# The last head of a cached-attention decode step in single-column products, with the output as four rows

## The chip, the cores and the metric

The kernel runs on one core of a Trainium2 chip. The metric is the device time of one execution in microseconds; each kernel was run several times, and medians are quoted. The profile's span is about 1.8 us shorter than the quoted time of the same execution in nearly all runs. All positions ("at 2511.9 us") are microseconds from the start of a span.

## The reference, cut to what matters

One token attends to a cache of 65,536 keys and values in each of 32 heads; a small gated feed-forward block is mixed in.

```python
B, Sq, D = 1, 1, 512
H, Sk, Dh = 32, 65536, 128              # k_cache, v_cache: (1, 32, 65536, 128) bf16, 512 MiB each

q = (x @ wq) in heads
p = softmax(einsum("bhqd,bhkd->bhqk", q, k_cache) * Dh**-0.5)
a = einsum("bhqk,bhkd->bhqd", p, v_cache) -> (1, 1, H*Dh) @ wo
b = (silu(x @ w_gate) * (x @ w_up)) @ w_down
g = sigmoid((x * gate_w).sum(-1))
out = g * a + (1 - g) * b               # (1, 1, 512)
```

## The kernel before

K and V stream through three slots of 8 MB in SBUF. Each head has two chunks (`CH = 2`), so there are 64 chunks, 0 to 63; chunks 62 and 63 are the last head. For a chunk, VectorE multiplies K by the broadcast q, TensorE (PE) sums over the head dimension with an identity as stationary operand ("score sums"), ScalarE takes the exponentials. Then V is weighted in one of two ways.

For all chunks but the very last, the probabilities are stationary, four columns at a time, and V streams through as 512 columns. That gives a 4 x 512 result of which four 1 x 128 pieces are wanted; `diagonal` picks them:

```python
    def pv(n):
        ...
        last = CH - 2 if h == H - 1 else CH - 1
        mms(("pv", s, n % 2, c == 0, c == last), O_ps,
            [(P_sb[n % 2][:, g : g + VB], v[:, g : g + VB, :].rearrange("p a b -> p (a b)"))
             for g in range(0, KPP, VB)], ...)          # 64 products of 512 columns
        if c == last:
            act("O_sb", O_sb, O_ps, ACT.Copy, ["O_ps"], ["O_sb"])
            pending.append(h)
```

For chunk 63 V itself is stationary and one column of probabilities streams through, 256 times; V arrives in five pieces, so the work can follow the loads. Then comes the end of the kernel:

```python
    V_END = [KPP // 2, KPP // 4, KPP // 8, KPP // 16, KPP // 16]    # 128, 64, 32, 16, 16 columns
    ...
    load("k", n, [EK] * (KPP // EK))
    load("v", n, V_END)
    turn_outputs(1)
    rows("b_ps", wd, ..., hT, "hT", range(FT))          # 56 single-column products
    diagonal()
    for i, j in enumerate(range(0, KPP, EK)):           # the last four blocks of scores
        block(n, j, EK)
        if i == 0:
            ...
            rows("a_ps", wo, ..., M, "M", range(H))     # 128 single-column products
        ...
    for m in V_END:
        mms(("c", at), m_c[:, 0:1],
            [(v[:, j, :], P_sb[n % 2][:, j : j + 1]) for j in range(at, at + m)], ...)
        if at == 0:
            norm(h, H)
        at += m
    dve("o_last", lambda: nc.vector.tensor_scalar_mul(o_last, m_c[:, 0:1], tot[:, h:H]), ...)
    rows("l_ps", wo_last, ..., o_last, "o_last", [0])   # 4 single-column products
    dve("out_sb", ...)                                  # [128, 4]
    dma("out", out[0, 0].rearrange("(p b) -> p b", b=OT), out_sb, ["out"], ["out_sb"])
```

The projections read their weights with a stride of four elements, so that the 512 outputs stand as 128 partitions x 4, and the output leaves as 128 pieces of 8 bytes:

```python
    def rows(key, w_v, names, cols, cname, ks):
        ... [(w_v[:, k, bass.ds(b, P, OT)], cols[:, k : k + 1]) for k in ks] ...   # b in 0..3
```

The softmax here doesn't subtract the row's maximum and nothing guards it: scores larger than these inputs give would overflow.

## Time and profile before

| before | value | where |
|---|---|---|
| time, first 3 runs | 2521.22 us median (2519.79 to 2521.41) | runs |
| DMA | 1088 MB at 432 GB/s, 99.7% of 16 engines' span | page, part 3 |
| last score sum starts | 2506.13 us | timeline |
| last piece of V landed | 2511.90 us | semaphore records |
| last single-column product starts | 2514.50 us | timeline |
| output issued, landed | 2515.62, 2518.59 us | timeline, semaphore records |

The kernel is a stream of loads with work behind it. So the reading starts with the DMA queues, from the page of the kernel before (queue and kind: packets, MB, share of the 16 engines' span):

```profile
span 2519.9 us, 15461 instructions
...
DMA packets 20903, 1088.04 MB, mean 432 GB/s; under 512 B 2450, under 2 KB 2580, under 8 KB 2836
## 3 DMA queue, kind: packets, MB, share of 16 engines
q1 hardware_dynamic: 20880, 1087.78, 99.7%
q8 instruction: 13, 0.21, 0.0%
```

The stream fills the engines. What a change at the end can win is the time from the last landing to the end. This is the last stretch of the chain of waits before (start, length, what; times in us):

```profile
2503.27 3.24 PE S_ps_102 L269 x15
2506.51 3.19 PE m_c L251 x128
2509.70 0.23 PE m_x L251 x2
2509.93 1.51 PE m_c L251 x58
2511.44 1.22 issue
2512.66 2.02 PE m_c L251 x70
...
2514.71 0.23 DVE o_last L588
...
2515.07 0.28 PE m_x L279 x4
...
2515.38 0.22 DVE out_sb L593
```

The first three lines say that PE was late: its score sums ended at 2506.5, when the first 128 columns of V had been there since 2502.2, and the 128 products that need them came only then. The line "1.22 issue" is a pause in the middle of a run of equal products; no semaphore ends it. The last V piece landed during that pause (2511.90), and 2.6 us later PE started its last product. The wait of the queue that issued the output, from the waits view (waited for: us in total, times, longest):

```profile
SPq L179 <- DMA out_dram<-out_sb: 2.6, 1, 2.6
```

With the issue itself that is 2.97 us from issue to landing, for 1 KB.

### The profile page before, as it was taken

The numbers are of one execution on the slowest core, as the hardware profiler recorded it, in microseconds if no ns is written. First come the engines' busy times: TensorE is split into PE (matmuls) and PEld (weight loads), VectorE is DVE, ScalarE is ACT, GpSimd is POOL, SyncE is SP. The second block draws the span as 40 slices with busy tenths as digits, with TensorE's granted clock in tenths as the row PEclk, the third lists the DMA queues.
The fourth block names the chain that finished last, engine by engine and source line by source line (L and its number), as shares of the span: only waits on it lengthen the run. The fifth ranks groups of instructions, "written<-read, shape, count | busy, mean of one in ns | idle before, by whom it ended". The sixth has DMA issues, their size and how long they took to land.

```text
span 2519.9 us, 15461 instructions
## 1 busy us (share of the span) xinstructions
PE 1980.9 (79%) x9115; PEld 410.4 (16%) x5153; DVE 1268.7 (50%) x290; ACT 97.9 (4%) x402; POOL 1.9 (0%) x9
## 2 busy tenths in 40 slices
PE   4787877877878778778787787787787877877888
PEld 1111111111111111111111111111111111111113
DVE  3455455464554554644645536446455455464454
ACT  0000000000000000000000000000000000000000
POOL 0000000000000000000000000000000000000000
PEclk8888988989889889899899899898988988989998
DMA  9999999999999999999999999999999999999998
GB/s 423 431 432 433 434 435 435 433 435 437 433 434 433 434 433 435 436 436 433 434 435 435 433 434 433 434 434 437 434 436 433 434 437 433 434 433 433 433 431 361
DMA packets 20903, 1088.04 MB, mean 432 GB/s; under 512 B 2450, under 2 KB 2580, under 8 KB 2836
## 3 DMA queue, kind: packets, MB, share of 16 engines
q1 hardware_dynamic: 20880, 1087.78, 99.7%
q8 instruction: 13, 0.21, 0.0%
q14 instruction: 6, 0.05, 0.0%
q10 hardware_dynamic: 4, 0.00, 0.0%
HBM read 1087.77 MB, written 0.00 MB: 432 GB/s over the span
## 4 chain that ended last, share of the span: by engine, by line
DMA 44%; PE 41%; DVE 13%; ACT 1%; issue 0%; another core or an unknown queue 0%; SPq 0%; DVEq 0%; ACTq 0%
PE O_ps L251 18%; DMA slot_67<-in_A_k_cache_dram 16%; DMA slot_65<-in_A_k_cache_dram 14%; DMA slot_66<-in_A_k_cache_dram 14%; PE S_ps_101 L269 11%; PE S_ps_102 L269 9%; DVE slot_67 L338 4%; DVE slot_66 L338 4%; DVE slot_65 L338 3%; DVE S_sb_82 L363 2%; PE m_c L251 1%; PE S_ps_101 L279 1%; PE m_x L279 1%; ACT P_sb_83 L288 1%; DMA slot_65<-in_A_wq_dram 0%; PE S_ps_102 L279 0%
## 5 line engine op out<-in xcount | busy, mean ns | idle before, releaser
L338 DVE TENSOR_TENSOR slot_67<-slot_67,q_bc_79 128x16384 bf16<-128x16384 bf16 (+1 forms) x28 | 208.2, 7469 | 143.8 <-DMA slot_67<-in_A_k_cache_dram 143.8
L363 DVE TENSOR_REDUCE S_sb_82<-S_ps_102 128x128 f32<-128x1024 f32 (+1 forms) x67 | 78.8, 1177 | 392.8 <-PE S_ps_102 L269 392.8
L338 DVE TENSOR_TENSOR slot_65<-slot_65,q_bc_78 128x16384 bf16<-128x16384 bf16 x22 | 190.2, 8689 | 146.9 <-DMA slot_65<-in_A_k_cache_dram 146.9
L338 DVE TENSOR_TENSOR slot_66<-slot_66,q_bc_78 128x16384 bf16<-128x16384 bf16 (+1 forms) x24 | 190.6, 7978 | 136.7 <-DMA slot_66<-in_A_k_cache_dram 121.2
L338 DVE TENSOR_TENSOR slot_66<-slot_66,q_bc_79 128x16384 bf16<-128x16384 bf16 x20 | 172.9, 8689 | 119.9 <-DMA slot_66<-in_A_k_cache_dram 119.9
L338 DVE TENSOR_TENSOR slot_65<-slot_65,q_bc_79 128x16384 bf16<-128x16384 bf16 x20 | 172.9, 8689 | 119.1 <-DMA slot_65<-in_A_k_cache_dram 119.1
L338 DVE TENSOR_TENSOR slot_67<-slot_67,q_bc_78 128x16384 bf16<-128x16384 bf16 x20 | 172.9, 8689 | 117.3 <-DMA slot_67<-in_A_k_cache_dram 117.3
L269 PE MATMUL S_ps_101<-slot_67,ident 128*128 128x512 bf16 x680 | 191.3, 450 | 0.0
L269 PE MATMUL S_ps_101<-slot_65,ident 128*128 128x512 bf16 x651 | 187.1, 458 | 0.0
L269 PE MATMUL S_ps_101<-slot_66,ident 128*128 128x512 bf16 x650 | 185.3, 455 | 0.0
L251 PE MATMUL O_ps<-slot_67,P_sb_83 128*4 128x512 bf16 x704 | 155.9, 383 | 27.9 <-ACT P_sb_83 L288 18.3
L251 PE MATMUL O_ps<-slot_65,P_sb_83 128*4 128x512 bf16 x704 | 155.2, 381 | 19.6 <-ACT P_sb_83 L288 19.6
L251 PE MATMUL O_ps<-slot_66,P_sb_84 128*4 128x512 bf16 x704 | 153.7, 379 | 19.3 <-ACT P_sb_84 L288 19.3
L251 PE MATMUL O_ps<-slot_65,P_sb_84 128*4 128x512 bf16 x640 | 139.7, 379 | 18.3 <-ACT P_sb_84 L288 18.3
L251 PE MATMUL O_ps<-slot_67,P_sb_84 128*4 128x512 bf16 x640 | 139.7, 379 | 18.3 <-ACT P_sb_84 L288 18.3
L251 PE MATMUL O_ps<-slot_66,P_sb_83 128*4 128x512 bf16 x640 | 139.7, 379 | 17.5 <-ACT P_sb_83 L288 17.5
L269 PE MATMUL S_ps_102<-slot_67,ident 128*128 128x512 bf16 x680 | 152.4, 382 | 0.0
L269 PE MATMUL S_ps_102<-slot_65,ident 128*128 128x512 bf16 x651 | 143.9, 379 | 0.0
L269 PE MATMUL S_ps_102<-slot_66,ident 128*128 128x512 bf16 x650 | 143.9, 379 | 0.0
L279 PE MATMUL S_ps_101<-slot_65,ident 128*128 128x512 bf16 x21 | 12.8, 608 | 134.5 <-DVE slot_65 L338 134.5
L279 PE MATMUL S_ps_101<-slot_66,ident 128*128 128x512 bf16 x22 | 13.1, 597 | 130.5 <-DVE slot_66 L338 130.5
L279 PE MATMUL S_ps_101<-slot_67,ident 128*128 128x512 bf16 x24 | 13.9, 580 | 125.4 <-DVE slot_67 L338 125.4
(89 smaller groups left out, 702.8 us busy)
## 6 DMA issues: line engine op xcount, KB each, us to landing
slot_66<-in_A_k_cache_dram SPq DMA_DIRECT2D x4, 2048.0 KB, 24.5
slot_67<-in_A_k_cache_dram SPq DMA_DIRECT2D x4, 2048.0 KB, 29.0
slot_65<-in_A_wq_dram SPq DMA_DIRECT2D x1, 4096.0 KB, 12.3
slot_66<-in_A_wo_dram SPq DMA_DIRECT2D x1, 4096.0 KB, 32.5
slot_65<-in_A_v_cache_dram SPq DMA_DIRECT2D x1, 4096.0 KB, 20.5
slot_65<-in_A_v_cache_dram SPq DMA_DIRECT2D x1, 2048.0 KB, 24.9
slot_65<-in_B_w_gate_dram SPq DMA_DIRECT2D x1, 1792.0 KB, 34.7
slot_65<-in_B_w_up_dram SPq DMA_DIRECT2D x1, 1792.0 KB, 38.4
```

What stands on the lines that cost most here:

```text
L251: ins = nc.tensor.matmul(out_ap, lhsT=a, rhs=b, start=start and i == 0, stop=stop and i == len(pairs) - 1,)
L269: ins = nc.tensor.add_instruction(mybir.InstMatmult(name=nc.get_next_instruction_name(), engine=mybir.EngineType.PE, ins=[nc.tensor.lower_ ...
L279: ins = nc.tensor.matmul(out_ap, lhsT=a, rhs=b, start=first, stop=last)
L288: "ACT", key, lambda: nc.scalar.activation(out=out_ap, in_=in_ap, func=func, **kw),
L338: "products", lambda: nc.vector.tensor_tensor(out=w, in0=w, in1=q_rep, op=ALU.mult),
L363: lambda: nc.vector.tensor_reduce(out=S_sb[b][:, :m], in_=S_ps[r][:, :m, :], axis=AXIS.X, op=ALU.add),
```

## The change

Intent: let PE finish sooner after the last landing, and let V's slot come free sooner. Four things change. (1) Chunk 62 is done in single-column products too, in three groups, and accumulates with chunk 63, so the last head has no diagonal. (2) Both projections move ahead of the last score sums. (3) The output is four rows of 128 (256 bytes each): the scaled last head is copied into four columns of a 128 x 16 zero matrix `Z` (column q of the q-th block of four), four products of 128 columns give a 4 x 128 result, and the part that was ready earlier is transposed to that shape ahead of time. (4) As a consequence the projections read contiguous weights. The diff also moves the row sums and the normalization of the earlier heads within the programs of PE and VectorE.

```diff
+    rest4 = sb("rest4", [OT, P], f32)
+    ident_f = sb("ident_f", [P, P], f32)
+    Z = sb("Z", [P, OT * OT], bf16)
-    out_sb = sb("out_sb", [P, OT], bf16)
+    out_sb = sb("out_sb", [OT, P], bf16)
...
-                    [(w_v[:, k, bass.ds(b, P, OT)], cols[:, k : k + 1]) for k in ks],
+                    [(w_v[:, k, P * b : P * (b + 1)], cols[:, k : k + 1]) for k in ks],
...
-        pv(n)
+        if n < N - 2:
+            pv(n)
+        else:
+            column(n, [KPP // 2, KPP // 4, KPP // 4])
...
+    turn_outputs(0)
     turn_outputs(1)
-    rows("b_ps", wd, units(ws, 0, WO), hT, "hT", range(FT))
-    diagonal()
+    rows("b_ps", wd, units(ws, 0, WO), hT, "hT", range(FT), m_x, "m_x")
+    rows("a_ps", wo, units(ws, WO, WL), M, "M", range(H), m_sp, "m_sp")
     for i, j in enumerate(range(0, KPP, EK)):
...
+            mms("rest_ps", m_sp[:OT, :P], [(rest, ident_f)], ["rest", "ident_f"], ["m_sp"])
+            act("rest4", rest4, m_sp[:OT, :P], ACT.Copy, ["m_sp"], ["rest4"])
...
-    rows("l_ps", wo_last, units(ws, WL, WL + D), o_last, "o_last", [0])
+    mms(
+        "l_ps", m_x[:OT, :P],
+        [(Z[:, OT * q : OT * (q + 1)], wo_last[:, 0, P * q : P * (q + 1)]) for q in range(OT)],
+        ["Z"] + units(ws, WL, WL + D), ["m_x"],
+    )
...
-    dma("out", out[0, 0].rearrange("(p b) -> p b", b=OT), out_sb, ["out"], ["out_sb"])
+    dma("out", out[0, 0].rearrange("(i p) -> i p", p=P), out_sb, ["out"], ["out_sb"])
```

More of the change, by code (lines that the diff above doesn't have):

```diff
@@ L148 @@
     rest = sb("rest", [P, OT], f32)
+    rest4 = sb("rest4", [OT, P], f32)
+    ident_f = sb("ident_f", [P, P], f32)
+    Z = sb("Z", [P, OT * OT], bf16)
     o_row = sb("o_row", [H, Dh], bf16)
     M = sb("M", [P, H], bf16)
-    o_last = sb("o_last", [P, 1], bf16)
-    out_sb = sb("out_sb", [P, OT], bf16)
+    out_sb = sb("out_sb", [OT, P], bf16)
     S_ps = [psum.tile([P, HK, R], f32, name=f"S_ps{i}") for i in range(2)]
@@ L226 @@
     op("DVE", "oT0", lambda: nc.vector.memset(oT, 0.0), writes=["oT"])
+    op("DVE", "Z0", lambda: nc.vector.memset(Z, 0.0), writes=["Z"])
     op("DVE", "rowsum0", lambda: nc.vector.memset(rowsum, 0.0), writes=["rowsum"])
@@ L239 @@
     select("ident", ident, ones_b, "ones_b", [[-1, P]], 1)
+    select("ident_f", ident_f, ones, "ones", [[-1, P]], 1)
     select("pick", pick, ones[0:VB, 0:VB], "ones", [[-1, VB]], 1)
@@ L381, in pv @@
         s = where["v", n]
-        last = CH - 2 if h == H - 1 else CH - 1
         v = view(s, 0, KPP, Dh)
         mms(
-            ("pv", s, n % 2, c == 0, c == last), O_ps,
+            ("pv", s, n % 2, c == 0, c == CH - 1), O_ps,
             [
@@ L393, in pv @@
             [("P_sb", n % 2, u) for u in range(RS)] + units(s, 0, SLOT), ["O_ps"],
-            start=(c == 0), stop=(c == last),
+            start=(c == 0), stop=(c == CH - 1),
         )
-        if c == last:
+        if c == CH - 1:
             act("O_sb", O_sb, O_ps, ACT.Copy, ["O_ps"], ["O_sb"])
@@ L403, in diagonal, with column @@
         mms(
-            ("diagonal", h == H - 1), m_c[:, 0:1],
+            "diagonal", m_c[:, 0:1],
             [(O_sb[:, j * Dh : (j + 1) * Dh], pick[:, j : j + 1]) for j in range(VB)],
-            ["O_sb", "pick"], ["m_c"], stop=(h < H - 1),
+            ["O_sb", "pick"], ["m_c"],
         )
-        if h < H - 1:
-            act("o_all", o_all[:, h : h + 1], m_c[:, 0:1], ACT.Copy, ["m_c"], [("o_all", h)])
+        act("o_all", o_all[:, h : h + 1], m_c[:, 0:1], ACT.Copy, ["m_c"], [("o_all", h)])
+    def column(n, pieces, at=0):
+        s = where["v", n]
+        v = view(s, 0, KPP, Dh)
+        for m in pieces:
+            mms(
+                ("c", n, at), m_c[:, 0:1],
+                [(v[:, j, :], P_sb[n % 2][:, j : j + 1]) for j in range(at, at + m)],
+                [("P_sb", n % 2, u) for u in range(at // EK, -(-(at + m) // EK))]
+                + units(s, at * Dh, (at + m) * Dh),
+                ["m_c"], start=(n == N - 2 and at == 0), stop=(n == N - 1 and at + m == KPP),
+            )
+            at += m
     def hidden():
@@ L456, in gate, with rows @@
         )
-    def rows(key, w_v, names, cols, cname, ks):
+    def rows(key, w_v, names, cols, cname, ks, bank, bname):
         group(
@@ L463, in rows @@
                 (
-                    m_x[:, b : b + 1],
-                    [(w_v[:, k, bass.ds(b, P, OT)], cols[:, k : k + 1]) for k in ks],
+                    bank[:, b : b + 1],
+                    [(w_v[:, k, P * b : P * (b + 1)], cols[:, k : k + 1]) for k in ks],
                 )
@@ L468, in rows, with sum_ps @@
             ],
-            names + [cname], ["m_x"],
+            names + [cname], [bname],
         )
-    def norm(h0, h1):
+    def sum_ps(h0, h1):
         w = CH * RS
@@ L475, in norm @@
             ["ones", "rowsum"] + [("rowsum", i) for i in range(h0 * w, h1 * w)], ["m_x"])
+    def norm(h0, h1):
+        w = CH * RS
         dve(
@@ L523 @@
         for j in range(0, KPP, m):
+            if n == N - 2 and j == 2 * m:
+                sum_ps(0, H - 1)
             block(n, j, m)
@@ L529 @@
                     diagonal()
-            elif n == N - 2 and j + m == KPP:
-                norm(0, H - 1)
-                outputs()
             while len(todo) > 1:
@@ L539 @@
         if n == N - 2:
-            turn_outputs(0)
-        pv(n)
+            norm(0, H - 1)
+            outputs()
+        if n < N - 2:
+            pv(n)
+        else:
+            column(n, [KPP // 2, KPP // 4, KPP // 4])
     n, h = N - 1, H - 1
@@ L553 @@
     load("v", n, V_END)
+    turn_outputs(0)
     turn_outputs(1)
-    rows("b_ps", wd, units(ws, 0, WO), hT, "hT", range(FT))
-    diagonal()
+    rows("b_ps", wd, units(ws, 0, WO), hT, "hT", range(FT), m_x, "m_x")
+    rows("a_ps", wo, units(ws, WO, WL), M, "M", range(H), m_sp, "m_sp")
     for i, j in enumerate(range(0, KPP, EK)):
-        block(n, j, EK)
-        if i == 0:
+        if i == 1:
             dve("rest", lambda: nc.vector.tensor_scalar_mul(rest, m_x[:, :OT], ngval),
                 ["m_x", "ngval"], ["rest"])
-            rows("a_ps", wo, units(ws, WO, WL), M, "M", range(H))
-        if i == 2:
             dve(
@@ L566 @@
                 lambda: nc.vector.scalar_tensor_tensor(
-                    out=rest, in0=m_x[:, :OT], scalar=gval, in1=rest, op0=ALU.mult, op1=ALU.add
+                    out=rest, in0=m_sp[:, :OT], scalar=gval, in1=rest, op0=ALU.mult, op1=ALU.add
                 ),
-                ["m_x", "gval", "rest"], ["rest"],
+                ["m_sp", "gval", "rest"], ["rest"],
             )
+        if i == 2:
+            mms("rest_ps", m_sp[:OT, :P], [(rest, ident_f)], ["rest", "ident_f"], ["m_sp"])
+            act("rest4", rest4, m_sp[:OT, :P], ACT.Copy, ["m_sp"], ["rest4"])
+        block(n, j, EK)
         while len(todo) > 1:
@@ L573 @@
     gather()
-    s = where["v", n]
-    v = view(s, 0, KPP, Dh)
-    at = 0
-    for m in V_END:
-        mms(
-            ("c", at), m_c[:, 0:1],
-            [(v[:, j, :], P_sb[n % 2][:, j : j + 1]) for j in range(at, at + m)],
-            [("P_sb", n % 2, u) for u in range(at // EK, -(-(at + m) // EK))]
-            + units(s, at * Dh, (at + m) * Dh),
-            ["m_c"], start=False, stop=(at + m == KPP),
-        )
-        if at == 0:
-            norm(h, H)
-        at += m
-    dve("o_last", lambda: nc.vector.tensor_scalar_mul(o_last, m_c[:, 0:1], tot[:, h:H]),
-        ["m_c", ("tot", h)], ["o_last"])
-    rows("l_ps", wo_last, units(ws, WL, WL + D), o_last, "o_last", [0])
+    column(n, V_END[:1])
+    sum_ps(h, H)
+    norm(h, H)
+    column(n, V_END[1:], V_END[0])
+    dve(
+        "Z",
+        lambda: nc.vector.tensor_scalar_mul(
+            Z[:, :: OT + 1], m_c[:, 0:1].to_broadcast([P, OT]), tot[:, h:H]
+        ),
+        ["m_c", ("tot", h)], ["Z"],
+    )
+    mms(
+        "l_ps", m_x[:OT, :P],
+        [(Z[:, OT * q : OT * (q + 1)], wo_last[:, 0, P * q : P * (q + 1)]) for q in range(OT)],
+        ["Z"] + units(ws, WL, WL + D), ["m_x"],
+    )
     dve(
@@ L593 @@
         lambda: nc.vector.scalar_tensor_tensor(
-            out=out_sb, in0=m_x[:, :OT], scalar=gval, in1=rest, op0=ALU.mult, op1=ALU.add
+            out=out_sb, in0=m_x[:OT, :P], scalar=gval[:OT, :], in1=rest4,
+            op0=ALU.mult, op1=ALU.add,
         ),
-        ["m_x", "gval", "rest"], ["out_sb"],
+        ["m_x", "gval", "rest4"], ["out_sb"],
     )
-    dma("out", out[0, 0].rearrange("(p b) -> p b", b=OT), out_sb, ["out"], ["out_sb"])
+    dma("out", out[0, 0].rearrange("(i p) -> i p", p=P), out_sb, ["out"], ["out_sb"])
     op("SP", "end", None, reads=["out"])
```

## The prediction

> **What bounds the kernel.** DMA. The page's DMA-queue part: 1088 MB at a mean 432 GB/s, the queue's packets filling 99.7% of the 16 engines; the slice row shows DMA at 9 in every slice but the last. PE is 79% busy and DVE 50%, but neither sets the pace. The change moves no byte out of this stream, so only what follows the last V landing, or starves the stream, can change the time.
>
> **The end of it, from the timeline, the windows and the semaphore records.** The last five pieces of V land at 2502.20, 2507.04, 2509.47, 2510.69 and 2511.90 us. PE is behind them: its last score sums start at 2502.9 and end at 2506.5, because 128 projection products (4.4 us, from 2488.2) and a half-clock stretch stood in front of the second block. It then does 256 single-column products at about 26 ns each, and pauses inside them: the chain of waits shows 1.22 us of "issue" from 2511.44, a pause that no semaphore ends. The DMA records have a 16,384-byte instruction packet from 2510.31 to 2511.24. The Trainium skill ("Runtime: NRT & Kernel Launch", Instruction fetch mechanics) says an engine's instructions come in 16 KiB blocks of 256 through the sequencer's own DMA queue; so I read the pause as an instruction fetch (inferred, not shown). The last product therefore starts at 2514.50, 2.6 us after the last V landing. Then: scaling (0.22), four products, final sum (0.22), issue at 2515.62, landing at 2518.59 (2.97 us), end at 2519.9.
>
> **What the change does, costed.**
> - Chunk 62: 64 products of 512 columns (15.5 us, 2466.2 to 2481.7) become 256 single-column products, estimated 6.7 us at 26 ns. V's slot comes free about 8 us earlier, so the last V loads are issued earlier. Worth about 0: the queue was already full (DMA share near 1.0 from 2460 to 2508).
> - The projections (1.9 and 4.4 us) move ahead of the last sums, into a hole where PE waits for K. The last sums should end at 2500.5 to 2504.5, and the first columns wait for V rather than V for them.
> - The diagonal (1.0 us) goes; a small transpose comes, off the path.
> - About 370 more PE instructions (384 added for chunk 62, 16 removed): the block boundary moves. An estimate by 256s puts it near the start of the second column group, where PE waits for V anyway, and the next near the last four products. It also means one or two more fetches, each of which delays one DMA engine by about 0.9 us (the spread of a landing grew from 2.0 to 3.1 us after the fetch at 2447); I expect other engines than the latest ones, so no later last landing.
> - End: last product at about 2512.5 (-2.0). Four products of 128 columns at half clock and a final sum over 128 elements instead of 4: +0.4. Output as four rows of 256 B instead of 128 pieces of 8 B: -0.5, a guess; most of the 2.97 us is the write's receipt (the skill's "DMA: Bandwidth & Descriptors", Anatomy of one DMA, says the same).
>
> Sum: about -2.1 us, 2519.1 us. This is 0.1%.
>
> **What would show it.** Chain of waits: no "issue" piece inside the last columns; DMA landing, then 16 columns. Last V landing still at 2511.9 +- 0.3. Last column to output issue 1.5 us (1.12 before). Output landing 2.2 to 2.7 us.
>
> **What would make it wrong.** A fetch pause in the last 32 columns or before the last four products (+1 to +2 us); a fetch hitting the latest DMA engine (+0.9); the scatter of the three runs before (1.6 us) is as large as the gain.
>
> Chances: faster by over 2% 0.005, within 2% 0.99, slower 0.005. 2519.1 us, range 2517.2 to 2521.0.

## More of the kernel before

PE's program is a loop over heads 1 to 30, three heads a round; head 0 and the last head are written out.

## The result, and the profile after

| | before | after |
|---|---|---|
| time, 4 runs each | 2521.18 us median (2519.79 to 2521.41) | 2518.43 us median (2518.11 to 2518.69) |
| span of the profile | 2519.9 us | 2517.0 us |
| last score sum starts | 2506.13 | 2501.54 |
| last piece of V issued, landed | 2483.52, 2511.90 | 2471.53, 2512.55 |
| last single-column product starts | 2514.50 | 2513.02 |
| output issued, landed | 2515.62, 2518.59 | 2514.50, 2515.69 |

The ratio of the fast runs is 0.999 (95% interval 0.9973 to 1.0008): the same at the 2% that counts here. Ratios are the mean time of one kernel's fast runs over the mean of the other's fast runs of the same rounds, so they are not quite the ratio of the medians quoted. The 2.75 us between the medians is small but larger than the scatter of the runs after, and the slowest run after is below the fastest run before. The runs after also scatter less: 0.6 us against 1.6 us.

The page after:

```profile
span 2517.0 us, 15837 instructions
...
DMA packets 20769, 1088.07 MB, mean 432 GB/s; under 512 B 2314, under 2 KB 2444, under 8 KB 2700
## 3 DMA queue, kind: packets, MB, share of 16 engines
q1 hardware_dynamic: 20744, 1087.78, 99.8%
q8 instruction: 15, 0.25, 0.0%
```

The stream is as full as before, and two more blocks of instructions were fetched (15 packets against 13). The end of the chain of waits after:

```profile
2471.53 41.02 DMA slot_65<-in_A_v_cache_dram
2512.55 0.05 issue
2512.60 0.60 PE m_c L255 x16
...
2513.23 0.24 DVE Z L606
...
2513.51 0.60 PE m_x L255 x4
...
2514.14 0.34 DVE out_sb L618
```

The chain now hangs on the load of V: it lands at 2512.55, then come 16 columns (0.60), the scaling (0.24), four products (0.60) and the final sum (0.34). No "issue" piece stands inside the last columns any more. The output's wait in the waits view:

```profile
SPq L181 <- DMA out_dram<-out_sb: 0.8, 1, 0.8
```

That is 1.19 us from issue to landing in place of 2.97. Of the 2.9 us between the two spans, 1.1 us is the earlier issue and 1.8 us the faster landing.

### The profile page after: what moved, and what is told of

It reads as the page before. It is cut to its first block, busy times and chain, and to the rows that moved or that the text cites. A ratio compares the mean times of both kernels' runs of the same rounds, so it can differ in the third digit from the quotient of the medians.

```text
span 2517.0 us, 15837 instructions
## 1 busy us (share of the span) xinstructions
PE 1966.3 (78%) x9301; PEld 409.7 (16%) x5339; DVE 1268.6 (50%) x291; ACT 97.8 (4%) x402; POOL 2.2 (0%) x10
## 3 DMA queue, kind: packets, MB, share of 16 engines
q1 hardware_dynamic: 20744, 1087.78, 99.8%
## 4 chain that ended last, share of the span: by engine, by line
DMA 46%; PE 39%; DVE 13%; ACT 1%; issue 1%; another core or an unknown queue 0%; SPq 0%; DVEq 0%; ACTq 0%
PE O_ps L255 17%; DMA slot_67<-in_A_k_cache_dram 16%; DMA slot_65<-in_A_k_cache_dram 14%; DMA slot_66<-in_A_k_cache_dram 14%; PE S_ps_103 L273 10%; PE S_ps_104 L273 8%; DVE slot_67 L342 4%; DVE slot_66 L342 4%; DVE slot_65 L342 3%; DMA slot_65<-in_A_v_cache_dram 2%; DVE S_sb_82 L367 2%; PE m_c L255 1%; PE S_ps_103 L283 1%; DMA slot_65<-in_A_wq_dram 1%; ACT P_sb_83 L292 0%
## 5 line engine op out<-in xcount | busy, mean ns | idle before, releaser
L255 PE MATMUL O_ps<-slot_67,P_sb_83 128*4 128x512 bf16 x704 | 155.7, 382 | 28.1 <-ACT P_sb_83 L292 18.3
L255 PE MATMUL O_ps<-slot_66,P_sb_84 128*4 128x512 bf16 x704 | 153.7, 379 | 19.3 <-ACT P_sb_84 L292 19.3
L255 PE MATMUL O_ps<-slot_65,P_sb_83 128*4 128x512 bf16 x640 | 139.7, 379 | 18.3 <-ACT P_sb_83 L292 18.3
L255 PE MATMUL O_ps<-slot_65,P_sb_84 128*4 128x512 bf16 x640 | 139.7, 379 | 18.3 <-ACT P_sb_84 L292 18.3
L255 PE MATMUL O_ps<-slot_67,P_sb_84 128*4 128x512 bf16 x640 | 139.7, 379 | 18.3 <-ACT P_sb_84 L292 18.3
L255 PE MATMUL O_ps<-slot_66,P_sb_83 128*4 128x512 bf16 x640 | 139.8, 379 | 17.5 <-ACT P_sb_83 L292 17.5
```

What stands on the lines that cost most here:

```text
L255: ins = nc.tensor.matmul(out_ap, lhsT=a, rhs=b, start=start and i == 0, stop=stop and i == len(pairs) - 1,)
```

## The experiments

Twelve kernels were run, five times each, every set with nine fresh runs of the kernel before on the same chip; those medians were 2521.25, 2521.43 and 2521.17 us. So times of different sets may be compared to about 0.3 us. Every kernel's verdict against before was "same" at 2%; the differences below are between medians, and their mechanism is read in the traces. This table has what decides each, from one profile of each kernel (us; "last score sum" is the start of the last one, and PE is early enough when that is near 2502.5, where the first piece of V lands):

| kernel | median of 5 | range | last score sum | last V landed | last column | output issue to landing |
|---|---|---|---|---|---|---|
| b_same | 2521.28 | 2519.62 to 2521.99 | 2505.36 | 2512.10 | 2514.13 | 3.02 |
| b_pad | 2522.27 | 2520.01 to 2522.81 | 2508.20 | 2512.16 | 2515.19 | 2.95 |
| b_rows | 2518.38 | 2518.14 to 2520.04 | 2501.46 | 2512.24 | 2512.71 | 1.18 |
| b_rows_str | 2520.22 | 2518.61 to 2520.86 | 2506.13 | 2511.89 | 2514.47 | 1.18 |
| a_cols | 2520.30 | 2519.94 to 2520.63 | 2501.84 | 2512.37 | 2512.84 | 3.20 |
| a_out8 | 2520.47 | 2520.17 to 2520.80 | 2501.64 | 2512.54 | 2513.01 | 3.11 |
| a_late | 2518.51 | 2518.30 to 2519.40 | 2505.60 | 2512.19 | 2512.85 | 1.18 |
| a_pv | 2520.22 | 2519.88 to 2520.33 | 2505.54 | 2512.12 | 2514.37 | 1.18 |
| a_pv_pad | 2518.38 | 2518.37 to 2518.61 | 2503.36 | 2512.08 | 2512.95 | 1.18 |
| a_pad30 | 2518.22 | 2518.14 to 2518.47 | 2501.73 | 2512.09 | 2512.55 | 1.18 |
| a_fine | 2518.36 | 2518.30 to 2518.54 | 2500.83 | 2512.18 | 2512.43 | 1.18 |
| a_roll5 | 2522.68 | 2522.46 to 2522.91 | 2505.87 | 2516.69 | 2517.15 | 1.18 |

### Which part: the output's form

Theory: the landing of the output is the larger part. Rival: the gain is PE's earlier end. Two kernels, one from each side. `b_rows` is the kernel before with the four rows alone (`rest4`, `ident_f`, `Z`, contiguous projection weights, the new `l_ps` and output). `a_cols` is the kernel after with the old ending:

```diff
-[(w_v[:, k, P * b : P * (b + 1)], cols[:, k : k + 1]) for k in ks]
+[(w_v[:, k, bass.ds(b, P, OT)], cols[:, k : k + 1]) for k in ks]
-Z, l_ps of 4 x 128 columns, out as "(i p) -> i p"
+o_last, rows("l_ps", ...), out as "(p b) -> p b"
```

> The kernel before with the four-row output alone (transposed rest, Z, four products of 128 columns, output as four rows of 256 B). Theory (the output form is the larger part of the gain): the issue comes about 0.4 us later, the landing takes 1.2 instead of 2.97 us, so 1.2 to 1.5 us faster than before, about 2519.8. The pause inside the last columns stays. Rival (the gain is the earlier end of the last products, the output form is worth only the 0.1 us left): within 0.4 us of before.

> The kernel after with the output in columns as before (128 pieces of 8 B). Theory: landing 2.9 to 3.0 us from issue instead of 1.19, issue about 0.5 us earlier; 1.2 to 1.5 us slower than after, about 2519.8. Rival: under 0.4 us from after.

`a_cols` took 2520.30 us, 1.9 us more than after: landing 3.20 us instead of 1.19, issue 0.28 us earlier. The theory holds and the size is larger than expected. The waits view of `a_cols`:

```profile
SPq L182 <- DMA out_dram<-out_sb: 2.8, 1, 2.8
```

`b_rows` took 2518.38 us. It is as fast as the whole change, where 1.2 to 1.5 us of gain was expected, in four of five runs; the fifth took 2520.04. The output's form alone does not explain that: in its profile the pause is gone from the chain, which hangs on V:

```profile
2482.04 30.20 DMA slot<-in_A_v_cache_dram
2512.28 0.60 PE m_c L255 x16
```

A shorter pause of 0.40 us is left inside the second column group, but three pieces of V land after it, so it costs nothing (timeline: start, length, engine, line, operation; the bracket is the idle time before it):

```profile
2509.06 0.35 PE L255 MATMUL m_c<-P_sb,slot 128*128 128x1 bf16 x8 [0.40 <-issue]
```

### Why the output lands sooner

The old output differs from the new in the number of pieces (128 against 4), their size (8 against 256 bytes), and in the partitions they leave from. `a_out8` keeps the four partitions and the whole computation, and cuts the rows into 8-byte pieces (wrong values):

```diff
-out[0, 0].rearrange("(i p) -> i p", p=P), out_sb
+out[0, 0].rearrange("(a i p) -> i a p", i=OT, p=4), out_sb.rearrange("i (a p) -> i a p", p=4)
```

> The kernel after with its four rows stored as 128 pieces of 8 B in a shuffled order (wrong values on purpose), from the same four partitions. Theory (number and size of the pieces make the old output's landing slow, not the 128 partitions or 16 engines): landing 2.5 us or more after the issue, 1.3 us or more slower than after. Rival (number of engines or partitions): landing 1.2 to 1.5 us, time as after.

Landing 3.11 us after the issue, and 2520.47 us in all. The pieces make the old output slow, not the 128 partitions. Their number and their size change together here and are not separated. The wait of the queue:

```profile
SPq L181 <- DMA out_dram<-out_sb: 2.8, 1, 2.8
```

### Why `b_rows` gained more: the projections' weights

`b_rows` also reads contiguous weights, since its outputs stand in another order. `b_rows_str` undoes only that:

```diff
-[(w_v[:, k, P * b : P * (b + 1)], cols[:, k : k + 1]) for k in ks]
+[(w_v[:, k, bass.ds(b, P, OT)], cols[:, k : k + 1]) for k in ks]
```

> Before with the four-row output alone, but with the projections' weights read with a stride of 4 elements as before (wrong values on purpose). Theory (with the contiguous weights a projection product costs 25 instead of 33 ns, and the single-column stretch of 128 becomes 3.2 instead of 4.2 us[...]): the 184 projection products take 1.5 us longer, the last sums end 1.5 to 5 us later than in the kernel with contiguous weights, and the time is 0.7 to 2 us more, 2519 to 2520.5, with more scatter. Rival (only the output's form counts): 2518.4 as with contiguous weights.

The 128 products in the tile view (instruction, count: shortest/median/longest ns, first and last start), first with contiguous weights (`b_rows`), then with the stride (`b_rows_str`):

```profile
L283 PEld LDWEIGHTS m_x<-M,slot x128: 95/95/98, 2486.1 to 2489.4; 128*128 128x128 bf16 x128
```

```profile
L283 PEld LDWEIGHTS m_x<-M,slot x128: 112/118/118, 2487.3 to 2491.7; 128*128 128x128 bf16 x128
```

From first to last start it is 3.3 us against 4.4 us. The matmuls themselves start 25 ns apart against 33 (median); the kernel before has 33 ns too, with the clock full throughout. The profile of `b_rows_str` has the late score sums (2506.13) and the pause in the columns again:

```profile
2509.93 1.46 PE m_c L255 x56
2511.38 1.19 issue
2512.58 2.07 PE m_c L255 x72
```

Its time went up by 1.8 us, its range is 2518.6 to 2520.9. So the contiguous weights were worth no less than the output's form, by which `b_rows_str` is 1.2 us faster than before. How much of it is the shorter products and how much the clock is not separated: between 2483 and 2497 it stood at half for 10 us in the profile of `b_rows_str`, and not at all in that of `b_rows`. The length of the stretch alone does not decide it: in `a_late`, below, the same 128 products with contiguous weights also took 3.2 us (from 2489.0 in the chain), and the clock fell at 2491.8.

### The pause: every 256th instruction

Numbering the PE instructions that the two traces record from 0, the pause before stands in front of number 14,404. After, PE pauses in front of 13,892 (3.2 us, inside chunk 62's columns), 14,148 (3.3 us, inside the attention projection) and 14,660 (1.0 us, at the start of the second column group). All four numbers lie a multiple of 256 apart, and for each the DMA records hold a 16,384-byte packet of the instruction queue; PE goes on 1.42 to 1.46 us after that packet's end in all four. The 0.40 us in `b_rows` are in front of 14,404 too, 1.43 us after a packet's end. Not every boundary stops PE: of the ten from 13,636 on in the profiles before and after, these four do. At 13,892 before, for one, the packet (counted back from the pause) had ended at 2486.48, and PE came there only at 2491.07. `b_pad` tests it on the kernel before, by 116 more PE instructions where PE is idle:

```diff
+        if n == N - 2:
+            dummies(58)        # 58 products ident x one column of ident, to an unused column
```

> The kernel before plus 58 useless single-column products (116 PE instructions) in front of chunk 62, where PE is idle. Theory (the pause inside the last columns is an instruction block that is not there yet, at every 256th instruction): the pause of 1.38 us leaves the 59th product of the second group and comes 116 instructions earlier, at the start of that group, where PE has other work behind it or waits for V; the last product starts 0.8 to 1.4 us earlier, and the run is that much faster than before. Rival (the pause belongs to the data or to the clock): pause where it was, time unchanged or slower.

The pause did leave the columns: in the profile the 128 products behind the second group's start run in one piece. It did not reappear at the boundary's new place either, at the start of that group: PE came there at 2511.85, and the packet had ended at 2509.61.

```profile
2508.58 3.19 PE m_c L251 x128
2511.99 3.38 PE m_c L251 x128
```

But the time did not improve: two runs at 2520.0 and 2520.3, three at 2522.3 to 2522.8. The profiled run (2522.8) had PE's clock at half in two stretches of 7 us in front of the last score sums, and these came 2 us later than before's (windows view; PEclk is the granted clock, after the busy times and counts):

```profile
core 0: us, PE busy (x) PEld busy (x) DVE busy (x) ACT busy (x) POOL busy (x), PEclk, DMA share, GB/s
2482.00:2489.00 7.00, 7.00 (x21) 1.19 (x7) 4.88 (x3) 0.00 (x0) 0.00 (x0) 0.52 1.01 431
2489.00:2492.00 3.00, 3.00 (x84) 2.79 (x82) 2.48 (x2) 0.35 (x2) 0.00 (x0) 1.00 1.12 481
2492.00:2499.00 7.00, 7.00 (x65) 1.65 (x50) 2.68 (x2) 0.00 (x0) 0.00 (x0) 0.51 0.96 410
```

So the position part of the theory held, and the time part did not: three runs of five are slower than the median of before, and the two others lie inside before's own range of that set (2519.62 to 2522.05). In the profiled run the trace shows PE too late even without the pause. `b_same`, the kernel before once more, shows the pattern as it is:

> The kernel before, unchanged, for a second profile of it. Theory (its end is set by PE, whose clock falls to half in stretches that depend on the phase of the run): last score sums end at 2504 to 2509 us, after the first V piece has landed, and times scatter over 1.5 us or more, 2519.6 to 2522. Rival (the end is set by the V landing and the scatter is DMA's): last sums end before 2502.5 and the last V landing moves with the time.

Late score sums (2505.36), a pause at the same instruction as in the first profile (1.65 us in the chain), and a range of 2.4 us. Why a run of before falls near 2519.6 or near 2521.5 was not traced for single runs; each kernel has one profile only.

`a_pad30` moves the boundaries of the kernel after by 60 instructions, into the first column group and into the last 30 products:

```diff
+        if n == N - 2:
+            dummies(30)
```

> The kernel after plus 30 useless products (60 PE instructions) in front of chunk 62. Theory: the block boundaries move to 60 instructions earlier in the program, into the first column group (102nd product or so of 128) and to the start of the last 32 products but a few; a pause of 1 to 3 us shows at the first, and one of up to 2 us at the second; 0.3 to 2 us slower than after. Rival: no change, as the 60 instructions run where PE is idle.

A miss: 2518.22 us, no slower than after. In its profile PE pauses in front of 13,892 and 14,148 again, 30 products earlier in the same work, and not at all at 14,660 and 14,916: their packets had ended at 2486.91 and 2508.64, and PE came there at 2505.04 and 2511.03. The boundaries in the columns did no harm to this PE, which was ahead of V.

### Chunk 62 and the projections

`a_late` puts the attention projection behind the first block of scores again:

```diff
-    rows("a_ps", ...)                       # ahead of the loop over the last blocks
     for i, j in enumerate(range(0, KPP, EK)):
         block(n, j, EK)
+        if i == 0:
+            rows("a_ps", ...)
```

> The kernel after with the 128 products of the attention projection behind the first block of the last scores again, as before. Theory (after is held by the V landing and has 4 us of room on PE): within 0.4 us of after, at most one slower run. Rival (the earlier projections are what buys the time): 1 us or more slower than after.

2518.51 us, with two runs at 2519.2 and 2519.4, one more than expected. The profiled run is that of 2519.4, but its span is 2516.8 us, as in the quicker runs (2516.4 to 2516.6), so most of its excess lies outside the span. The score sums were late by 4.1 us in its profile (2505.60). Its chain hangs on PE and not on V: the last 128 columns run in one piece, without a pause, and the last starts 0.66 us behind the last landing, against 0.47 after. The move is room, here just used up, and not time.

`a_pv` gives chunk 62 back to the wide products and the diagonal:

```diff
-        if n < N - 2:
-            pv(n)
-        else:
-            column(n, [KPP // 2, KPP // 4, KPP // 4])
+        pv(n)
...
+    diagonal()
```

> The kernel after with chunk 62 by the 64 wide products and the diagonal again (372 PE instructions fewer). Theory (held by the V landing): within 0.5 us of after; the earlier issue of the V loads buys nothing, their landings stay; one to two instruction fetches fewer ahead of the last landing, so the latest engine is at most as late, 3.0 to 3.5 us after the first. The block boundary falls back to the 59th product of the second group, and the pause there may cost up to 0.7 us. Rival (single-column products for chunk 62 are the gain): 1 us or more slower than after.

1.8 us slower, which is what the rival had said. With 372 PE instructions fewer, number 14,404 is again in the second column group, and another pause of 2.5 us, in front of 13,892, stands inside the attention projection ahead of the score sums, which are late:

```profile
2502.68 3.24 PE S_ps L273 x15
2509.33 1.40 PE m_c L255 x56
2510.73 1.75 issue
2512.48 2.08 PE m_c L255 x72
```

So there were two readings: the wide products are slower, or the instructions fell badly. `a_pv_pad` is the same kernel plus 58 useless products in front of chunk 62.

> The kernel with the wide products for chunk 62 (1.8 us slower than after), plus 58 useless products (116 PE instructions) in front of chunk 62. Theory (what the wide products lost is the pause at every 256th instruction, which stood inside the last columns): the boundary moves to the start of the second column group, no pause inside it, last product about 2513, time 2518.3 to 2518.9. Rival (the wide products end the scores too late, pause or not): stays at 2519.8 or more.

2518.38 us. More work made the kernel 1.8 us faster and as fast as after. The chain hangs on the V landing again, and the pause, still in front of number 14,404, has gone to the sum in front of the second column group, where PE has time. A short one of 0.27 us, in front of 14,660, now stands in the last columns (chain, then timeline):

```profile
2478.88 33.20 DMA slot<-in_A_v_cache_dram
2512.12 0.53 PE m_c L255 x14
2512.65 0.27 issue
2512.92 0.21 PE m_c L255 x2
```

```profile
2508.36 0.28 PE L255 MATMUL m_x<-rowsum,ones 128*128 128x8 f32 x2 [1.43 <-issue]
2508.50 3.11 PE L255 MATMUL m_c<-P_sb,slot 128*128 128x1 bf16 x112
```

This shows that the single-column form of chunk 62 was not needed for the gain, though its 256 products took 6.8 us of PE time (without the pause) against 14.0 us for the wide ones in `a_pv_pad`, and though V's first load was issued at 2464.2 instead of 2477.1. What the kernel without it lost, it lost by where the blocks of instructions end: the pause of 2.5 us in the projection is gone too, and the first score sum of chunk 63 starts 2.4 us earlier (2484.72 against 2487.08).

### What a fetch costs the stream

Each load has 16 completions in the semaphore records. Sorted, and counted from the first, those of three loads after show what fetches do; that a fetch packet runs on one of the DMA engines that carry K and V is inferred from them, as no record names an engine. Between the first line and the second lie the fetches at 2447.05 and 2467.35: two completions leave the crowd near 1.5 and stand at 2.71 and 3.04. During the third load comes the fetch at 2474.95: the entry at 2.09 is gone and one at 3.65 is new. The last V landings then stay 3.5 to 3.6 us behind the first:

```
K of chunk 62, first at 2436.51:  0.00 0.01 0.06 0.10 0.34 0.55 1.24 1.38 1.44 1.45 1.45 1.55 1.61 1.68 1.69 2.14
wo,            first at 2469.78:  0.00 0.01 0.05 0.06 0.33 0.55 1.38 1.43 1.44 1.44 1.56 1.66 1.69 2.09 2.71 3.04
K of chunk 63, first at 2474.97:  0.00 0.07 0.07 0.09 0.40 0.57 1.36 1.41 1.45 1.45 1.61 1.68 1.69 2.67 3.01 3.65
```

`a_roll5` makes many fetches out of the same work, by running only five rounds of PE's loop and writing out 15 heads more:

```diff
-    rounds = (H - 2) // BODY
+    rounds = 5                      # and dummies(28) in front of chunk 62, for the same alignment
```

> The kernel after with 5 rounds of the PE loop instead of 10: 15 more heads unrolled, about 6090 more PE instructions in the program for the same work, so about 24 more instruction fetches of 16 KB; 28 useless products bring the block boundaries at the end back to where they were. Theory (each fetch holds one DMA engine for about 0.9 us that it never makes up, because the stream is saturated): every engine is hit once or twice more, all landings of the last V piece come 1 to 1.7 us later, time 1 to 1.7 us more than after. Rival (a fetch costs its bytes alone, 24 x 16 KB at 432 GB/s = 0.9 us at most, and engines make it up): under 0.9 us more.

2522.68 us, 4.2 us slower than after, far outside both expectations. Page and chain:

```profile
span 2521.1 us, 15788 instructions
...
q8 instruction: 39, 0.64, 0.1%
```

```profile
2476.12 40.57 DMA slot<-in_A_v_cache_dram
2516.73 0.60 PE m_c L255 x16
```

24 more packets moved 0.4 MB, which is 0.9 us at 432 GB/s, but the last V landing came 4.1 us later than after (2516.69 against 2512.55), while the first completion of that piece came at 2508.89, no later than after (2509.05). Six completions of 16 stayed within 0.6 us of the first and two within 1.9; the other eight came 5.8 to 7.8 us behind it. So the fetches did not spread over all engines, and a delayed engine did not catch up. Why some were spared is open. The blocks of the loop itself are not fetched in each round: in the kernels before and after, no packet of that instruction queue (q8) lies between 315 and 2447 us.

### A smaller last piece

`a_fine` loads the last 16 columns of V as 8 and 8, in the hope of a version faster than both.

```diff
-    V_END = [KPP // 2, KPP // 4, KPP // 8, KPP // 16, KPP // 16]
+    V_END = [KPP // 2, KPP // 4, KPP // 8, KPP // 16, KPP // 32, KPP // 32]
```

> The kernel after with the last 16 columns of V loaded as 8 and 8. Theory (after the last landing PE has only the columns of the last piece to do): 8 columns less behind the last landing, 0.2 us faster than after, 2518.2. Rival (smaller pieces cost the DMA more than that): same or slower.

2518.36 us against after's 2518.43 in another set. The last columns take 0.39 us behind the landing instead of 0.60 in the profile, but the difference of the times is below what two sets can tell. It is inconclusive, and no version was found that is clearly faster than the kernel after.

## Why the prediction was right or wrong

The total was right: 2519.1 us predicted, 2518.43 measured, inside the range. Two of its terms were wrong in opposite directions, so part of the accuracy is luck.

- *DMA bounds it, only what follows the last landing counts.* Right: 99.8% of the engines' span after, and the chain ends with the V landing and 1.9 us of work.
- *Earlier V loads are worth about 0.* Right: the last piece was issued 12 us earlier (about 8 were predicted for the slot) and landed 0.65 us later.
- *The pause is an instruction fetch, and the boundary moves to the start of the second group and near the last four products.* Right: PE paused there for 1.0 us, behind a wait for V of 1.3 us, and the next boundary, 256 instructions on, fell on the four last products, where nothing was lost. The steps of 256 in the traces and `a_pv_pad` support it.
- *The score sums end at 2500.5 to 2504.5.* Right: the last one starts at 2501.54. That this mattered because of the earlier projections, as the text had it, was only half right: `b_rows` got there without that move, by contiguous weights and a full clock, and `a_late`, without the move, lost no time in its median though its sums were late. What cost time was lateness together with the pause (`a_pv`, `b_rows_str`), or more lateness alone (`b_pad`, 2508.20).
- *Last V landing at 2511.9 +- 0.3, because the fetches hit other engines than the latest.* Wrong by 0.65 us: after a fetch, a completion that was late already stood 1.6 us later (2.09 to 3.65). The risk was named, with 0.9 us a fetch.
- *Output as four rows: -0.5 us, a guess, landing in 2.2 to 2.7 us.* This step failed: the prediction took most of the 2.97 us for a cost that the form of the store does not change. The term was -1.8 us: the landing took 1.19 us, and `a_out8` shows that the 8-byte pieces were what took the rest. With the wider final products (+0.4 expected; last product to issue 1.48 us against 1.12, so +0.36) the ending gained 1.4 us instead of 0.1.
- *Last product at 2512.5 (-2.0 us).* It started at 2513.02 (-1.5), the 0.65 us of the landing.

## What to carry to other kernels

In a kernel that is bound by its loads, ask what stands between the last landing and the end, and look at the store itself: 1 KB in 8-byte pieces cost 1.9 us more than in four rows. When a run of equal instructions pauses with no semaphore behind it, number the instructions from pause to pause: if the distance is a multiple of 256, padding or cutting the program elsewhere moves it or removes it, and a change of the work may have won only by moving it. It need not cost time where the engine is ahead of its loads. Before unrolling a loop in a load-bound kernel, count the blocks: here 24 more of them cost 4.2 us.

## What the Trainium skill lacked or had wrong

- "Runtime: NRT & Kernel Launch", Instruction fetch mechanics: the blocks of 256 instructions (16 KiB) agree with the distances here. That crossing a boundary is "mostly hidden" held at six of the last ten boundaries in the profiles before and after, and not at the other four, where PE paused 1.0 to 3.3 us; and 24 more fetches made the kernel 4.2 us slower, so the page's preference for unrolling did not hold here either. It does not say what a fetch does to a full stream of loads: one completion of 16 stays late to the last load (by 1.6 us in the lines shown).
- "DMA: Bandwidth & Descriptors", Anatomy of one DMA: its fixed cost of about 2.0 us is given for the path through GpSimd, and it has none for a whole small store from the SP queue, which took 1.18 us for four rows of 256 B. It has no figure for a store in many tiny pieces: 2.95 to 3.20 us for 128 of 8 B.
- "SBUF — State Buffer", the note on cachelines: it has a stride of up to 8 bf16 elements for free. Stationary operands with a stride of 4 bf16 elements cost 33 ns a product against 25 ns contiguous, at full clock.
- "TensorE: Matmul & The Clock Gate", Part 1: it says that the clock follows how busy PE was, but not that single-column products do not keep it up. After, PE issued such products without a gap from 2460.8, and the clock fell to half at 2465.7, before the first pause (2466.8); before, they began at 2506.4, and it fell at 2510.2, ahead of the pause at 2511.4. In the windows view of the kernel after (PE and PEld busy 5.00 of 5 us, then PEclk 0.97, and 0.50 in the next 5 us):

```profile
2461.00:2466.00 5.00, 5.00 (x205) 5.00 (x202) 1.56 (x4) 0.35 (x2) 0.00 (x0) 0.97 1.04 448
2466.00:2471.00 5.00, 1.86 (x57) 1.57 (x54) 0.00 (x0) 0.09 (x1) 0.00 (x0) 0.50 0.95 403
```
